# Column sums of pk: from TensorE passes with a vector of ones to block transposes on VectorE and a trip through DRAM

## The chip, the cores and the metric

The kernel runs on one core of one Trainium2 chip. The metric is the device time of one execution in microseconds (us); the median of three runs of the kernel before is 577.03 us (576.88, 577.03 and 579.19).

## What is computed

Two independent inputs, A and B, each go through the same linear attention block with S = 2048 tokens, D = 640 and 32 heads of 20 columns; the two results stand side by side in the output. Cut to one input:

```python
qkv = x @ wqkv                                   # q, k, v by heads
phi = lambda t: where(t > 0, t + 1, exp(t)) + 1e-6
pq, pk = phi(q), phi(k)
kv = einsum("bhsd,bhse->bhde", pk, v)
z  = einsum("bhsd->bhd", pk)                      # sum of pk over the tokens
num = einsum("bhqd,bhde->bhqe", pq, kv)
den = einsum("bhqd,bhd->bhq", pq, z)[..., None] + 1e-6
out = (num / den) @ wo
```

The change concerns z: for each input 640 column sums of pk over 2048 tokens. They are needed as one number per partition: z as a tile of 128 x 5, where column c holds the sums of the columns 128c to 128c+127.

## The kernel before

All large products are split into a rounded high part and a low part of float32r and cost three matmuls each (hi x hi, hi x lo, lo x hi); the projections of k and the last product go through a Strassen-like scheme of seven products (`kprod`, `outmm`).

The first half of the program (to about 293 us) makes k and its sums for A, then for B. The tokens are taken in pairs p of 128-token tiles (`("p", p, n)`: product n of pair p) and in groups i of four tiles (`("g", i, s)`, `("h", i, s, n)`: the sum of x-transposed times pk for the slice s, accumulated in PSUM and added to the SBUF tiles gacc by `gacc_add`). pk of a tile n is made from ko by `phi_exp`, `phi_relu` (ACT), `phi_mix` (DVE, L496), `phi_hi` (ACT) and `phi_lo` (DVE, L512). `phi_z` sends the 128 x 640 tile of each n to DRAM with an accumulating DMA on GpSimd's queue (zd), so that after 16 tiles zd holds, for each of 128 partitions, partial column sums over 16 tiles.

Then, for each input, `kvmm` (L648) multiplies gacc with wv for six groups of heads into a PSUM bank (pskv), `kv_mask` (DVE, L655) masks it out of the bank, `kv_hi` and `kv_lo` split it, and `mmm` multiplies it with the split wo (`o_hi` on ACT, `o_lo` on DVE, with low's line L131). The products, m, go to DRAM (md), are loaded again and combined into sums (`form_sums1`, L726, and others) for the last product. For A this lies among the k work of B; for B it lies in the second half, at the start of which the q projections begin: `qmm(u, c)` computes 128 x 512 of q for the token group u, into a PSUM bank psq, in five steps k, and after each step `run("q", u, c, k)` performs what `at(...)` put there. Three PSUM banks have the tag "one"; psq and pskv both take from it.

The order of the work is written out by hand. In the first half, steps (TensorE work, in the order of the calls, some shifted by the table MOVED) are numbered, and jobs (the other engines' work and the DMAs) are placed behind a step, some shifted by the table SHIFT; `perform` emits all in the order of these positions, a job behind the earlier created ones of the same position. Every engine and every queue performs its own instructions in exactly this order. The DMAs of loads stand on SP's queue; an instruction that waits there holds all behind it.

The column sums before: `load_z` loads zd (128 x 640) into SBUF, `zmm` makes five matmuls of it with a vector of ones into a PSUM bank psz (L609; each shows as two passes), and `z_out` adds a constant and makes the sum s of the row. For A, `load_z` stands behind ("p", 9, 2), `zmm` is a step of its own before the sums of group 4, and `z_out` follows it. For B, `load_z` stands behind ("g", 7, 7), and `zmm` and `z_out` are put at ("q", 0, 1, 0), ahead of the second `kv_step`. z is first used by `qacc` (ACT, L825) for A at the first psq of the q work, and for B four token groups later.

Of the kernel before, what the change touches and what calls it, by code (L numbers as in the profile page):

```python
# [7 lines left out]
F32 = mybir.dt.float32  # L8
# [4 lines left out]
OP = mybir.AluOpType  # L13
# [3 lines left out]
EPS = 1e-6  # L17
# [51 lines left out]
}  # L69
GROUPS = [(0, 6), (6, 6), (12, 6), (18, 6), (24, 4), (28, 4)]  # L70

# [2 lines left out]
def tile_linear_attn_pair(ctx: ExitStack, tc: tile.TileContext, ins, out: bass.AP):  # L74
# [12 lines left out]
    nc = tc.nc  # L87
    P = 128
    S, D = ins[0]["x"].shape
    NC = D // P  # L90
    NT = S // P
# [7 lines left out]
    base = ctx.enter_context(tc.tile_pool(name="base", bufs=1))  # L99
    psums = ctx.enter_context(tc.tile_pool(name="psums", bufs=1, space=bass.MemoryType.PSUM, reuse_waits="tile"))  # L100

    def bank(name, tag="one"):
        return psums.tile([P, 512], F32, name=name, tag=tag, bufs={"one": 3, "a": 2, "e": 2, "small": 1}[tag])

    dram = ctx.enter_context(tc.tile_pool(name="dram", bufs=1, space=bass.MemoryType.DRAM))
# [42 lines left out]
    def at(slot, f, *a):  # L148
        todo.setdefault(slot, []).append((f, a))
# [7 lines left out]
    wst, whl = {}, {}  # L157

    def stage(name):
        return base.tile([P, D], F32, name=name, tag="wst", bufs=7)  # L160
# [69 lines left out]
            later(1, xq_lo, u, c)  # L230


    ones = base.tile([P, 1], F32)
    epst = base.tile([P, 1], F32)
    same = base.tile([P, P], F32R)
    mask = {}
# [1 line left out]
    nc.vector.memset(epst, EPS)  # L238

    def constants():  # L240
        nc.vector.memset(ones, 1.0)
        ij = base.tile([P, P], I32, name="ij", tag="kvt", bufs=3)
        nc.gpsimd.iota(ij, pattern=[[1, P]], base=0, channel_multiplier=-1)
        nc.vector.tensor_scalar(ij, ij, H - 1, None, op0=OP.bitwise_and)
        nc.vector.tensor_scalar(same, ij, 0.0, None, op0=OP.is_equal)
        for nh in (6, 4):
            v = base.tile([P, DH * nh], F32, name=f"v{nh}", tag="kvt", bufs=3)
            m = base.tile([P, DH * nh], F32, name=f"mask{nh}")
            nc.gpsimd.iota(v, pattern=[[0, DH], [-DH, nh]], base=0, channel_multiplier=1,
                           allow_small_or_imprecise_dtypes=True)  # L250
            nc.vector.tensor_scalar(m, v, 0.0, None, op0=OP.is_ge)
            nc.vector.scalar_tensor_tensor(m, v, float(DH - 1), m, op0=OP.is_le, op1=OP.mult)
            mask[nh] = m
# [58 lines left out]
    def step(name, f, *a, after=()):  # L312
        assert name not in place, name
        place[name] = len(steps)
        steps.append((len(steps), -1, name, f, a, after))
# [7 lines left out]
    def job(name, spot, f, *a, after=()):  # L323

        spot = (place[spot] if isinstance(spot, tuple) else spot) + SHIFT.get(name, 0)
        jobs.append((spot, len(jobs), name, f, a, after))
        return spot
# [9 lines left out]
    pk, ko, zacc, gacc, kps, wf = {}, {}, {}, {}, {}, {}  # L337
# [107 lines left out]
    def prods(p, *ns):  # L445
        b = p // (NT // 2)
        for n in ns:
            after = [(k, p, x) for x in LEFT[n] for k in ("xh", "xl")]
            after += [("wf", b, i, k) for i in RIGHT[n] for k in "hl"]
            after += {2: [("c0", p)], 4: [("c2", p)], 5: [("c4", p)], 6: [("q4", p), ("p", p, 1)]}.get(n, [])  # L450
            step(("p", p, n), kprod, p, n, after=after)
# [127 lines left out]
    def gsums(i, ss, js, tags={}):  # L579
        b, g = divmod(i, NG)  # L580
        for s in ss:
            n = begun.get((i, s), 0)
            begun[i, s] = n + len(js)
            tag = tags.get(s, "one")
            step(("g", i, s) if n + len(js) == 4 else ("h", i, s, n), gsum, i, s, js, tag, n,
                 after=[(k, 4 * i + j) for j in js for k in ("nh", "nl", "ph", "pl")] + before.get((i, s), []))
            before[i, s] = [("h", i, s, n)]
# [7 lines left out]
            job(("gacc", i, s), ("g", i, s), gacc_add, i, s, after=after)  # L595


    zz, zps, md, wvt, wot, kvt, kvp, mps = {}, {}, {}, {}, {}, {}, {}, {}
    written = []

    def load_z(b):
        wst["z", b] = base.tile([P, D], F32, name="zs", tag=f"wo{'hl'[b]}", bufs=2)
        nc.sync.dma_start(wst["z", b], zacc[b])

    def zmm(b):
        x = wst["z", b]
        zps[b] = bank("psz", "small")
        for c in range(NC):
            nc.tensor.matmul(zps[b][:, c:c + 1], x[:, c * P:(c + 1) * P], ones, start=True, stop=True)  # L609

    def z_out(b):
        z = base.tile([P, NC], F32, name="z", tag="z", bufs=2)
        s = base.tile([P, 1], F32, name="zs", tag="zs", bufs=2)
        nc.vector.tensor_scalar(z, zps[b][:, :NC], S * EPS, None, op0=OP.add)
        nc.vector.tensor_reduce(s, z, axis=mybir.AxisListType.X, op=OP.add)
        nc.vector.tensor_scalar(s, s, EPS, EPS / 4, op0=OP.mult, op1=OP.add)
        zz[b] = z, s

    def z_step(b):
        zmm(b)  # L620
        z_out(b)

    def load_v(b, g):
        h0, nh = GROUPS[g]
# [327 lines left out]
    LG = NU - 1  # L952
# [41 lines left out]
    t = wst["k", 0, 0] = stage("wst")  # L994
# [24 lines left out]
    for n in first:  # L1019
        p, c = divmod(n, 2)  # L1020
# [56 lines left out]
    for i in range(NU):  # L1077
        P0, P1 = 2 * i + 1, 2 * i + 2
        if i == 0:
            gsums(i, range(2 * NC), range(4))  # L1080
        elif i in (NG - 1, LG):

            prods(P0, 0, 1, 3, 2)
            gsums(i, [0, 1], [0, 1])
            prods(P0, 4)
            gsums(i, [2], [0, 1])
            prods(P0, 5, 6)
            if i == LG:
                step(("switch",), switch, after=[("st", P0, k) for k in range(3)])
            gsums(i, range(3, 6), [0, 1], {3: "a", 4: "e", 5: "small"})  # L1090
            gsums(i, range(6), [3])
            gsums(i, range(6), [2])
            gsums(i, range(6, 2 * NC), range(4))
        elif i == NG:

            both(P0 - 1, P0)
            kvs(0)
            prods(P0, 4)
            kvs(1)
            prods(P0, 5, 6)  # L1100
            kvs(2, 3, 4, 5)
            gsums(i, range(3), [0, 1])
            step(("z",), zmm, 0, after=[("zl",)])
            gsums(i, [0], [2, 3])
            gsums(i, [1], [2, 3])
            gsums(i, [2], [2, 3])
            gsums(i, [3], range(4))
            ms(0)
            prods(P1, 0, 1, 3, 2)
            gsums(i, [4], range(4))  # L1110
            ms(1)
            prods(P1, 4)
            gsums(i, [5], range(4))
            ms(2)
            prods(P1, 5, 6)
            gsums(i, [6, 7], range(4))
            ms(3)
            gsums(i, [8], range(4))
            ms(4)
            gsums(i, [9], range(4))  # L1120
        else:
            both(P0, P1)
            gsums(i, [0], [0, 1])
            prods(P1, 4)
            gsums(i, [1, 2], [0, 1])
            prods(P1, 5, 6)
            gsums(i, range(3), [2, 3])
            gsums(i, [3], range(4))
            if i == NG + 1:
                ms(5)  # L1130
            gsums(i, range(4, 2 * NC), range(4))
# [4 lines left out]
    def h(i, s):  # L1136
        return ("h", i, s, 0)
# [18 lines left out]
    a = x_parts(1, "A2", ("c", 0, 4), [("t", 3)])  # L1156
    stores(1, 1, a + 2, ["A2"])
    a = x_parts(2, "A1", ("c", 2, 4), [("t", 4)])
    stores(2, 0, a + 2, ["A1"])
    x_parts(2, "B1", ("c", 2, 4), [("t", 5)])  # L1160
    a = x_parts(2, "A2", ("c", 3, 0), [("t", 5)])
    b = x_parts(2, "A5", ("c", 3, 0), [("t", 4), ("xh", 2, "A2")])
# [4 lines left out]
    for i in range(NU):  # L1167
# [6 lines left out]
        else:  # L1174
# [6 lines left out]
            q = P0 + 2  # L1181
# [72 lines left out]
    for g in range(NGR):  # L1254
        job(("v", g), (("p", 8, 0), ("p", 8, 1), ("p", 8, 3), ("p", 8, 2), ("p", 9, 0), ("p", 9, 1))[g], load_v, 0, g)
        a = job(("kt", g), ("kv", g), kv_mask, 0, g, after=[("kv", g)])
        job(("o", g), a, load_o, 0, g)
        a = job(("kvh", g), a, kv_hi, 0, g, after=[("kt", g)])
        job(("kvl", g), a + 1, kv_lo, 0, g, after=[("kvh", g)])
        a = job(("woh", g), (h(4, 2), ("g", 4, 3), ("p", 10, 2), ("g", 4, 5), ("g", 4, 6), ("g", 4, 8))[g], o_hi, 0, g,  # L1260
                after=[("o", g)])
        job(("wol", g), a + 0.5, o_lo, 0, g, after=[("woh", g)])
        for k, t in enumerate("ae"):
# [3 lines left out]
                       [("g", 5, 8), ("p", 14, 4)], [("g", 5, 9), h(6, 1)], ("g", 6, 4),  # L1267
                       [(0, ("p", 13, 1)), (2, ("p", 14, 0)), (6, ("p", 14, 3)), (4, h(6, 0)), (1, ("g", 6, 0)),
                        (3, ("g", 6, 2)), (5, ("g", 6, 4)), (7, ("g", 6, 5)), (8, ("p", 15, 4)), (9, ("g", 7, 0))]))
    job(("zl",), ("p", 9, 2), load_z, 0, after=[("zs", n) for n in range(NT)])  # L1270
    job(("zo",), ("z",), z_out, 0, after=[("z",)])
    job(("zl1",), ("g", LG, 7), load_z, 1, after=[("zs", n) for n in range(NT, NN)])


    for c in range(NC):
        job(("wq", c), ("p", 15, c + 1), load_w, "q", 0, c)
        a = job(("wqh", c), ("g", LG, c), wq_hi, 0, c, after=[("switch",), ("wq", c)])
# [3 lines left out]
        a = job(("xqh", c), ("g", LG, 5 + c), xq_hi, 0, c, after=[("xq", c), ("xraw", c)])  # L1281
# [8 lines left out]
           form_load, 0, i)  # L1290
    for i in range(6, 10):
        at(("q", 1, i - 5, 4) if i < 9 else ("q", 1, 4, 0), form_load, 0, i)
    at(("q", 0, 1, 0), z_step, 1)


    for g in range(NGR):
# [137 lines left out]
```

## Time and profile before

| | |
|---|---|
| median of three runs | 577.03 us |
| the profiled execution | a span of 581.2 us from the first to the last instruction; no other time of its own is given |
| TensorE (PE) busy | 571.2 us, 98% |
| VectorE (DVE) busy | 436.6 us, 75% |
| ScalarE (ACT) busy | 334.0 us, 57% |
| GpSimd (POOL) busy | 84.2 us, 14% |
| mean granted clock of TensorE | 0.993 |
| moved by DMA | 123.59 MB, 213 GB/s in the mean |

In rows of the timeline the first two numbers are the start and the duration in us; the form is out<-in by the program's names; what stands in brackets is the idle time of the engine before the instruction, and what ended it. SPq and POOLq rows are DMA issues on the queues of SyncE and GpSimd; "landing" is the time from an issue to the arrival of the data. In a row of waits stand the sum in us, the number of times and the longest. In a row of windows stand, behind the stretch, its length, the busy time (and count) of PE, PEld, DVE, ACT and POOL, the granted clock of TensorE as a share of the full one, the busy share of the DMA engines, and GB/s.

### The profile page before, as it was taken

The page shows a single profiled execution, that of the slowest core. Times are in us where ns is not written, and L with a number is a line of the kernel's source. Part 1 is how long each engine was busy: PE and PEld are TensorE (multiplying, and loading weights), DVE is VectorE, ACT ScalarE, POOL GpSimd, SP SyncE. Part 2 cuts the span into 40 slices and gives each one's busy share as a digit, 9 for nine tenths or more (in the row PEclk, how much of TensorE's full clock was granted, in tenths as well). Part 3 has the DMA queues.
Part 4 walks back from the last instruction along what each step waited for, and adds up shares of the span by engine and source line. Part 5 has one row for each costly group of instructions (what it writes and reads, how often), then busy time and mean ns, then how long its engine had stood idle before and what let it go on. Part 6 is the DMA issues. An engine that isn't in the chain of part 4 may idle for free.

```text
span 581.2 us, 9643 instructions
## 1 busy us (share of the span) xinstructions
PE 571.2 (98%) x3541; PEld 541.1 (93%) x3541; DVE 436.6 (75%) x742; ACT 334.0 (57%) x625; POOL 84.2 (14%) x139
## 2 busy tenths in 40 slices
PE   9999999999999999989989999999999999999997
PEld 7999999999999999979978889898998989898897
DVE  6897698976675778768734698977799876767792
ACT  5955757562765774736534765744647454545541
POOL 0210132310012111323200101311011200001010
PEclk9999999999999999989999999999999999999999
DMA  8879599899986958968899884764273994122022
GB/s 291 239 160 258 116 259 334 178 378 347 303 205 160 250 130 193 306 200 241 225 314 304 277 287 164 272 199 161 67 255 112 389 375 153 68 65 91 0 91 91
DMA packets 70263, 123.59 MB, mean 213 GB/s; under 512 B 7560, under 2 KB 32520, under 8 KB 70216
## 3 DMA queue, kind: packets, MB, share of 16 engines
q1 hardware_dynamic: 57912, 83.25, 44.3%
q0 software_dynamic: 12160, 39.66, 24.9%
q8 instruction: 28, 0.46, 0.3%
q14 instruction: 19, 0.16, 0.1%
q10 hardware_dynamic: 144, 0.07, 0.0%
HBM read 73.60 MB, written 49.35 MB: 212 GB/s over the span
## 4 chain that ended last, share of the span: by engine, by line
PE 52%; DMA 3%; DVE 2%; issue 0%; SPq 0%; ACT 0%; DVEq 0%
PE pa L281 12%; PE psq L142 8%; PE psq L141 8%; PE psq L143 8%; PE pe L281 6%; PE psb L281 4%; PE psg L142 2%; PE psg L143 1%; PE psg L141 1%; DMA wst<-md 1%; DMA xqs<-in_A_xt 1%; DMA zs<-zd 1%; PE pskv L648 1%; PE psd L838 0%; PE psd L837 0%
## 5 line engine op out<-in xcount | busy, mean ns | idle before, releaser
L142 PE MATMUL psg<-pkl,xnh 128*128 128x320 f32 x320 | 99.9, 312 | 2.8 <-DVE pkl L512 2.8
L141 PE MATMUL psg<-pkh,xnh 128*128 128x320 f32 x320 | 99.7, 312 | 0.0
L143 PE MATMUL psg<-pkh,xnl 128*128 128x320 f32 x320 | 99.5, 311 | 0.0
L141 PE MATMUL psq<-xqh,wqh 128*128 128x512 f32 x200 | 79.0, 395 | 0.0
L142 PE MATMUL psq<-xql,wqh 128*128 128x512 f32 x200 | 78.7, 393 | 0.0
L143 PE MATMUL psq<-xqh,wql 128*128 128x512 f32 x200 | 78.6, 393 | 0.0
L142 PEld LDWEIGHTS psg<-pkl,xnh 128*128 128x128 f32 x320 | 60.7, 190 | 3.6 <-DVE pkl L512 3.6
L143 PEld LDWEIGHTS psg<-pkh,xnl 128*128 128x128 f32 x320 | 60.7, 190 | 0.0
L141 PEld LDWEIGHTS psg<-pkh,xnh 128*128 128x128 f32 x320 | 60.6, 190 | 0.0
L285 ACT ACTIVATE o<-pa 128x320 f32<-128x320 f32 x64 | 27.9, 438 | 44.7 <-PE pa L281 44.6
L817 DVE SCALAR_TENSOR_TENSOR pq<-eq,rq 128x512 f32<-128x512 f32 x40 | 27.6, 691 | 28.3 <-ACT rq L816 28.3
L504 POOL DMA_DIRECT2D zd<-ek x30 | 26.2, 874 | 139.7 <-DVE ek L496 62.9
L285 ACT ACTIVATE ko<-pa 128x320 f32<-128x320 f32 x52 | 22.5, 435 | 41.0 <-PE pa L281 41.0
L143 PEld LDWEIGHTS psq<-xqh,wql 128*128 128x128 f32 x200 | 38.0, 190 | 8.1
L141 PEld LDWEIGHTS psq<-xqh,wqh 128*128 128x128 f32 x200 | 37.9, 189 | 7.3
L142 PEld LDWEIGHTS psq<-xql,wqh 128*128 128x128 f32 x200 | 37.9, 189 | 7.2
L815 ACT ACTIVATE eq<-psq 128x512 f32<-128x512 f32 x40 | 23.8, 596 | 33.9 <-PE psq L143 31.5
L577 DVE TENSOR_TENSOR gacc<-psg,gacc 128x320 f32<-128x320 f32 x60 | 28.6, 486 | 8.1 <-PE psg L143 8.1
L372 ACT ACTIVATE ksh<-sx 128x512 fp32r<-128x512 f32 x26 | 16.3, 628 | 30.5 <-DVE sx L390 30.4
L508 ACT ACTIVATE pkh<-ek,epst 128x640 fp32r<-128x640 f32 x32 | 26.3, 829 | 12.4 <-DVE ek L496 12.4
L496 DVE SCALAR_TENSOR_TENSOR ek<-ek,ko 128x640 f32<-128x640 f32 x32 | 26.2, 822 | 8.3 <-ACT ko L493 6.5
L134 ACT ACTIVATE dah<-pq 128x1024 fp32r<-128x1024 f32 (+5 forms) x27 | 18.2, 708 | 20.4 <-DVE pq L849 20.4
(190 smaller groups left out, 1618.2 us busy)
## 6 DMA issues: line engine op xcount, KB each, us to landing
zd<-ek POOLq DMA_DIRECT2D x32, 320.0 KB, 5.2
out<-o POOLq DMA_DIRECT2D x28, 320.0 KB, 3.2
xql<-xd SPq DMA_DIRECT2D x24, 256.0 KB, 4.4
xn<-in_A_x SPq DMA_DIRECT2D x16, 320.0 KB, 4.8
xt<-in_B_xt_tiles SPq DMA_DIRECT2D x16, 320.0 KB, 5.1
xn<-in_B_x SPq DMA_DIRECT2D x16, 320.0 KB, 5.1
xqs<-in_A_xt SPq DMA_DIRECT2D x20, 256.0 KB, 5.7
xqs<-in_B_xt SPq DMA_DIRECT2D x20, 256.0 KB, 4.5
```

The lines of the kernel that those rows point to most:

```text
L134: nc.scalar.activation(hi, src, AF.Copy)
L141: nc.tensor.matmul(o, whi, xhi, start=first, stop=False)
L142: nc.tensor.matmul(o, whi, xlo, start=False, stop=False)
L143: nc.tensor.matmul(o, wlo, xhi, start=False, stop=last)
L281: nc.tensor.matmul(o, x, y, start=start and m == r == 0, stop=m == len(terms) - 1 and r == 2, skip_group_check=True)
L285: nc.scalar.activation(x, y, AF.Copy)
L496: nc.vector.scalar_tensor_tensor(ek[n], ek[n], 1.0, rk[n], op0=OP.min, op1=OP.add)
L504: nc.gpsimd.dma_start(zacc[b], e, accum_op=OP.add)
L508: nc.scalar.activation(pk[n][0], ek[n], AF.Identity, bias=epst)
L577: nc.vector.tensor_tensor(o, sums[i, s], o, op=OP.add)
L815: nc.scalar.activation(e, ps, AF.Exp)
L817: nc.vector.scalar_tensor_tensor(pq[u][:, c, :], e, 1.0, r, op0=OP.min, op1=OP.add)
```

## The change

The matmuls with ones go, with the vector of ones and the bank psz. In their place `z_turn` transposes the loaded 128 x 640 tile on DVE in blocks of 32 x 32 (20 columns of blocks, four rows), and a DVE sum over the 32 elements of each block row gives 128 x 20 partial sums. `z_store` writes these 10 KB to DRAM in one DMA, `z_back` reads them in four DMAs of 32 partitions, in runs of five elements (20 bytes), so that the four parts of a column's sum stand on one partition, and `z_out` adds the four, then does what it did before.

For A, `load_z` moves from ("p", 9, 2) to ("p", 11, 0), and the others stand behind ("p", 12, 3), ("g", 5, 3), ("p", 14, 1) and ("g", 7, 0); the step of `zmm` is gone from the list of steps, and its shift from MOVED. The shift of `z_out` of A in SHIFT, 1.19, stays. For B, `load_z` stays, `z_turn` takes the place of `zmm` at ("q", 0, 1, 0), and the rest is put at ("q", 0, 1, 4), ("q", 0, 3, 0) and ("q", 1, 2, 1). The transposed tile takes a buffer of the other wo tag, the sums one of the three buffers kvt.

```diff
     def load_z(b):
-        wst["z", b] = base.tile([P, D], F32, name="zs", tag=f"wo{'hl'[b]}", bufs=2)
-        nc.sync.dma_start(wst["z", b], zacc[b])
-
-    def zmm(b):
-        x = wst["z", b]
-        zps[b] = bank("psz", "small")
-        for c in range(NC):
-            nc.tensor.matmul(zps[b][:, c:c + 1], x[:, c * P:(c + 1) * P], ones, start=True, stop=True)
+        zt[b] = base.tile([P, D], F32, name="zs", tag=f"wo{'hl'[b]}", bufs=2)
+        nc.sync.dma_start(zt[b], zacc[b])
+
+    def z_turn(b):
+        t = base.tile([P, D], F32, name="zt", tag=f"wo{'lh'[b]}", bufs=2)
+        nc.vector.transpose(t, zt[b])
+        zt[b] = base.tile([P, 2, 4 * NC], F32, name="zr", tag="kvt", bufs=3)
+        nc.vector.tensor_reduce(zt[b][:, 0].rearrange("p (j c) -> p c j", j=4),
+                                t.rearrange("p (c j a) -> p c j a", c=NC, j=4), axis=mybir.AxisListType.X, op=OP.add)
+
+    def z_store(b):
+        zr[b] = dram.tile([4, 32, 4 * NC], F32, name=f"zr{b}")
+        nc.sync.dma_start(zr[b].rearrange("i b c -> (i b) c"), zt[b][:, 0])
+
+    def z_back(b):
+        for j in range(4):
+            nc.sync.dma_start(zt[b][32 * j:32 * (j + 1), 1].rearrange("b (i c) -> b i c", i=4),
+                              zr[b][:, :, NC * j:NC * (j + 1)].rearrange("i b c -> b i c"))
 
     def z_out(b):
...
-        nc.vector.tensor_scalar(z, zps[b][:, :NC], S * EPS, None, op0=OP.add)
+        nc.vector.tensor_reduce(z, zt[b][:, 1].rearrange("p (i c) -> p c i", i=4),
+                                axis=mybir.AxisListType.X, op=OP.add)
+        nc.vector.tensor_scalar(z, z, S * EPS, None, op0=OP.add)
...
-            step(("z",), zmm, 0, after=[("zl",)])
...
-    job(("zl",), ("p", 9, 2), load_z, 0, after=[("zs", n) for n in range(NT)])
-    job(("zo",), ("z",), z_out, 0, after=[("z",)])
+    job(("zl",), ("p", 11, 0), load_z, 0, after=[("zs", n) for n in range(NT)])
+    job(("zt",), ("p", 12, 3), z_turn, 0, after=[("zl",)])
+    job(("zw",), ("g", 5, 3), z_store, 0, after=[("zt",)])
+    job(("zb",), ("p", 14, 1), z_back, 0, after=[("zw",)])
+    job(("zo",), ("g", LG, 0), z_out, 0, after=[("zb",)])
...
-    at(("q", 0, 1, 0), z_step, 1)
+    at(("q", 0, 1, 0), z_turn, 1)
+    at(("q", 0, 1, 4), z_store, 1)
+    at(("q", 0, 3, 0), z_back, 1)
+    at(("q", 1, 2, 1), z_out, 1)
```

More of the change, by code (lines that the diff above doesn't have):

```diff
@@ L230, in round_xq @@
             later(1, xq_lo, u, c)
-    ones = base.tile([P, 1], F32)
     epst = base.tile([P, 1], F32)
@@ L240, in constants @@
     def constants():
-        nc.vector.memset(ones, 1.0)
         ij = base.tile([P, P], I32, name="ij", tag="kvt", bufs=3)
@@ L595, in gacc_jobs @@
             job(("gacc", i, s), ("g", i, s), gacc_add, i, s, after=after)
-    zz, zps, md, wvt, wot, kvt, kvp, mps = {}, {}, {}, {}, {}, {}, {}, {}
+    zz, zt, zr, md, wvt, wot, kvt, kvp, mps = {}, {}, {}, {}, {}, {}, {}, {}, {}
     written = []
     def load_z(b):
-        wst["z", b] = base.tile([P, D], F32, name="zs", tag=f"wo{'hl'[b]}", bufs=2)
-        nc.sync.dma_start(wst["z", b], zacc[b])
-    def zmm(b):
-        x = wst["z", b]
-        zps[b] = bank("psz", "small")
-        for c in range(NC):
-            nc.tensor.matmul(zps[b][:, c:c + 1], x[:, c * P:(c + 1) * P], ones, start=True, stop=True)
+        zt[b] = base.tile([P, D], F32, name="zs", tag=f"wo{'hl'[b]}", bufs=2)
[13 more added lines that the diff above has]
+                              zr[b][:, :, NC * j:NC * (j + 1)].rearrange("i b c -> b i c"))
     def z_out(b):
@@ L617, in z_out @@
         zz[b] = z, s
-    def z_step(b):
-        zmm(b)
-        z_out(b)
     def load_v(b, g):
```

2 rows, old and new, of the table MOVED are left out of this document.

## The prediction

> **What bounds the kernel now.** I read the page first (span and busy times), then the chain of waits of TensorE, then the timeline of PE, DVE, ACT and SP around the two places where the column sums z are made, then the granted clock there.
>
> ```profile
> span 581.2 us, 9643 instructions
> PE 571.2 (98%) x3541; PEld 541.1 (93%) x3541; DVE 436.6 (75%) x742; ACT 334.0 (57%) x625; POOL 84.2 (14%) x139
> ```
> ```profile
> PE psg L142 <- DVE pkl L512: 2.8, 1, 2.8
> PE psz L609 <- DMA zs<-zd: 1.4, 1, 1.4
> PE pskv L648 <- DMA wv<-in_B_wv: 0.7, 1, 0.7
> ```
>
> TensorE is busy 571.2 of 581.2 us, and these three waits are most of the rest. So the time is PE's own instructions plus its few stalls: an instruction taken from PE counts in full, unless PE then runs into something that its delay had hidden. The profiled execution spans 581.2 us and the median of the runs shown is 577.03, so I work out a difference within the profile and add it to 577.03. Below 0.5%, 2.9 us, a measurement of this kernel hardly tells a difference from none: its three runs lie 2.3 us apart.
>
> **The passes that go.** PE's timeline, first at z of input A, then at z of input B:
>
> ```profile
> 164.25 1.21 PE L609 MATMUL psz<-ones,zs 128*128 128x1 f32 x10
> 165.32 0.39 PE L141 MATMUL psg<-pkh,xnh 128*128 128x320 f32 x1
> ```
> ```profile
> 298.90 0.39 PE L143 MATMUL psq<-xqh,wql 128*128 128x512 f32 x1
> 299.13 0.40 PE L141 MATMUL psq<-xqh,wqh 128*128 128x512 f32 x1
> 299.60 0.40 PE L143 MATMUL psq<-xqh,wql 128*128 128x512 f32 x1
> 301.42 1.28 PE L609 MATMUL psz<-ones,zs 128*128 128x1 f32 x10 [1.42 <-DMA zs<-zd]
> 302.55 1.29 PE L648 MATMUL pskv<-gacc,wv 128*120 128x120 f32 x10
> 303.60 0.55 PE L141 MATMUL psq<-xqh,wqh 128*128 128x512 f32 x1
> 307.33 1.21 PE L648 MATMUL pskv<-gacc,wv 128*120 128x120 f32 x10
> 309.78 1.21 PE L648 MATMUL pskv<-gacc,wv 128*120 128x120 f32 x10
> ```
> ```profile
> 254.00:256.00 2.00, 2.00 (x10) 2.00 (x9) 0.74 (x3) 0.74 (x1) 1.09 (x2) 0.50 0.57 149
> 304.00:306.00 2.00, 2.00 (x6) 1.60 (x5) 0.45 (x2) 0.30 (x1) 0.00 (x0) 0.50 1.03 242
> ```
>
> At A the passes hold PE from 164.25 to 165.32: 1.07 us. Nothing there waits, and until 248 the list shows no wait of PE; the only gap is one of 0.1 us at 214 (below). So I count -1.07 us.
>
> At B PE is free at 301.42 - 1.42 = 300.0, waits for zs, makes z until 302.55, and then its clock falls: column PEclk of the last fence reads 0.50 for 304 to 306. Nine psq matmuls and no more run between 303.60 and 307.33, 3.73 us; at the full clock they start 0.23 apart (298.90, 299.13), 2.1 us. So z at B costs 1.42 + 1.13 + 1.63 = 4.2 us. How much of it comes back depends on what PE meets next.
>
> **What PE meets at B.** The same stretch on the other engines: the load of wv for the second kv product, and the path of the first wo tile through ACT and DVE.
>
> ```profile
> L626 SPq DMA_DIRECT2D wv<-in_B_wv x1: 328/328/328, 294.9 to 294.9; - x1
> DMA to landing us min/median/max: 5.4/5.4/5.4
> ```
> ```profile
> 306.37 0.74 ACT L677 ACTIVATE woh<-wo 120x640 fp32r<-120x640 f32 x1 [1.87 <-DMA wo<-in_B_wo]
> 307.14 0.83 DVE L131 TENSOR_TENSOR wol<-wo,woh 120x640 fp32r<-120x640 f32 x1 [2.32 <-ACT woh L677]
> 308.58 0.28 DVE L655 TENSOR_TENSOR kvt<-pskv,mask 120x120 f32<-120x120 f32 x1 [0.61 <-PE pskv L648]
> ```
>
> Without z, the second kv product needs wv, issued at 294.9 and landed 5.4 later: it starts at 300.4, not 302.55. From there PE needs 1.05 (302.55 to 303.60) for it, 2.1 for nine psq, 1.05 for the third kv product, and 0.7 each for the last three psq of one bank and the first three of the next: 306.0. Next is the fourth kv product, which before starts at 309.78. It writes the PSUM bank of the third, so it waits until DVE has masked that one (L655). DVE stands in its queue at wol, ahead of this mask; wol waits for woh, and woh for wo, which lands at 306.3 whatever PE does. So the mask can't start before 307.14 + 0.83 = 308.0 and ends near 308.2. A second delay lies before it: z_out of A now stands in DVE's queue between the gacc adds and the wql splits that free the slots for SP's loads; its four small instructions I price at 0.5 us on the landing of wo, between 0 and 0.8. The fourth kv product starts near 308.7 instead of 309.78: -1.1 us, with PE idle for 2.7 us from 306.0.
>
> The wait that takes the place costs clock as well. Two rows bear on that: after the wait of 2.8 us near 250 the clock stood at 0.50 in 254 to 256, and after 1.42 us of waiting and 1.13 us of 128x1 passes at 0.50 in 304 to 306. The new wait is as long as either, so I take the same loss, +1.63 us, which may also be 0. The Trainium skill, TensorE: Matmul & The Clock Gate, section Why this matters for your kernels, says there should be no idle gap over about 3 us between bursts; by that rule a gap of 2.7 us keeps the clock, and the sum would be 1.63 less. The trace speaks against it: 2.8 us were enough.
>
> **z_turn, new on DVE.** A transpose and a sum over 128x640, at step ("p", 12, 3) for A and behind the first psq bank for B. No row shows a DVE transpose. DVE's rows of 640 and the dearest row by length:
>
> ```profile
> L512 DVE SCALAR_TENSOR_TENSOR pkl<-ek,pkh 128x640 fp32r<-128x640 f32 x32 | 25.9, 820 | 4.4 <-ACT pkh L508 4.4
> L843 DVE RECIPROCAL rd<-psd 128x256 f32<-128x256 f32 x16 | 27.9, 1747 | 0.9 <-PE psd L838 0.9
> ```
> ```profile
> 205.40 0.68 DVE L131 TENSOR_TENSOR ksl<-sx,ksh 128x512 fp32r<-128x512 f32 x1
> 207.24 0.82 DVE L496 SCALAR_TENSOR_TENSOR ek<-ek,ko 128x640 f32<-128x640 f32 x1 [0.20 <-ACT ko L493]
> 210.10 0.49 DVE L288 TENSOR_TENSOR ko<-pe,ko 128x320 f32<-128x320 f32 x1 [2.03 <-ACT ko L285]
> 213.22 0.83 DVE L512 SCALAR_TENSOR_TENSOR pkl<-ek,pkh 128x640 fp32r<-128x640 f32 x1 [0.17 <-ACT pkh L508]
> ```
> ```profile
> 208.40 0.31 PE L281 MATMUL pa<-wfh,ksl 128*128 128x320 f32 x1
> 214.10 0.41 PE L142 MATMUL psg<-pkl,xnh 128*128 128x320 f32 x1
> ```
> ```profile
> 199.98 0.42 SPq L349 DMA_DIRECT2D xt<-in_B_xt_tiles  x1
> DMA to landing us min/median/max: 5.3/5.6/5.9
> ```
>
> I take 0.82 each, nearest in length, 1.64 for the pair; the ends are 0.5 and 1.75 each. At A the load of z stands in SP's queue behind the xt load of 199.98, so it is issued at 200.4 and lands, with the 5.6 of the zs loads before, at 206.0. z_turn stands ahead of the ksl of 205.40: it runs to 207.65, ksl to 208.3, and PE uses ksl at 208.40. It just fits. Behind come ko, ek, then ACT's pkh and the row of 210.10, whose idle time of 2.03 us takes up most of the delay. The end is tight: the pkl of 213.22 ends at 214.05 and PE takes it at 214.10. I count +0.2 us, between 0 and 1.5; if that cover is gone, a slower transpose is paid for in full here. At B the transposed sum ends near 303.1, two us ahead of the wait for wol, and costs nothing.
>
> **z_back, new on SP.** Its four DMAs stand between the last xn load of that stretch and the loads of md at step ("p", 13, 4). The same place before:
>
> ```profile
> 241.25 2.09 SPq L165 DMA_DIRECT2D wst<-md  x3
> ```
> ```profile
> 242.44 7.12 DMA wst<-md
> ```
> ```profile
> 249.66 0.49 DVE L726 TENSOR_TENSOR t<-wst 128x320 f32<-128x320 f32 x1 [3.62 <-DMA wst<-md]
> ```
> ```profile
> 251.47 0.42 PE L142 MATMUL psg<-pkl,xnh 128*128 128x320 f32 x1 [2.78 <-DVE pkl L512]
> ```
> ```profile
> L202 SPq DMA_DIRECT2D xd<-kal x16: 370/426/1038, 10.5 to 268.1; - x16
> ```
>
> This is the longest wait of PE: SP issues the md loads at once after the xn load, DVE stands at L726 until they have landed, the pkl behind it is late, PE waits 2.78 us. Each issue put ahead of them pushes all of this back. No row shows a DMA of 20-byte runs; the nearest short-run store, xd, takes SP 0.43 us, at most 1.04. Four issues are 1.7 us; part of that lies under the queue of transfers already in flight (7.12 us to land), so I count +1.5 us, from 0.5 to 4.2. The clock is lost here before and after, for nothing more. z_store of A (13 steps earlier) and the moved load of z lie where SP has time: zero. At B SP comes to z_back near 312 and may have to wait for z_store, issued after 306, to land: with landings of 5.4 to 7 us some 1.5 us, and 1.7 for the four issues. Behind it stands the xql load for the second q group:
>
> ```profile
> 314.22 0.37 SPq L219 DMA_DIRECT2D xql<-xd  x1
> DMA to landing us min/median/max: 6.9/6.9/6.9
> ```
> ```profile
> 325.73 0.40 PE L142 MATMUL psq<-xql,wqh 128*128 128x512 f32 x1
> ```
>
> Before it lands at 321.1 and is used at 325.73: 4.6 us of cover for 3.2, so zero, and up to 1 us if z_store lands late. z_out of B comes when nobody needs it yet: zero.
>
> **Sum.** -1.07 (A's passes) + 0.2 (DVE at 206) + 1.5 (md) - 1.1 (B) + 1.63 (clock at B) = +1.2 us: 582.4 for a profile, 578.2 us for the median.
>
> **The rivals.** *The clock holds*: the gap at B falls across two of the stretches over which the clock is judged. Then 578.2 - 1.6 = 576.6 us. Against it stand both rows of 0.50; for it, that the gap is only just as long. This is where the rule of the Trainium skill cited above, TensorE: Matmul & The Clock Gate, would put the time. *Nothing stands in the way at B*: wo lands earlier, or the mask isn't behind wol any more. Then the fourth kv product starts at 306.0, 3.8 us earlier than 309.78, and no clock is lost: -1.07 + 0.2 + 1.5 - 3.8 = -3.2, 573.8 us; 572.3 if the md wait also stays as it is. For it speaks that DVE had idle time there, against it ACT's 1.87 us of waiting for wo in a stretch whose DMA share is 1.03. *z_back costs its upper end*: one mechanism, SP's queue at 241.25. If the four issues with their short runs take 1.04 us each, md lands 4.2 us later and the wait of 2.78 becomes 7: +2.7 to the sum, 580.9 us. This decides from about 3.2 us on (sum over 2.9). For it speaks that the first md issue already takes SP over 1 us, a sign that the queue is full; against it, that a full queue also hides what is put into it.
>
> **How the numbers follow.** Forecast 0.42 (its own range 576.8 to 580.2, the ends of 0.2 and of z_out's 0.5 and 1 us of md), clock holds 0.16, nothing in the way 0.16, z_back dear 0.21, the rest 0.05 (a slow transpose at 206, some 1.5 to 3 us slower). Faster by over 0.5% (under 574.1) is the third case, 0.15; slower (over 579.9) is the fourth, most of the rest and the forecast's tail, 0.28; the same, 0.57. The range from 573.4 to 581.4 leaves out the outer parts of the third and fourth case.
>
> **What would show it.** Right: PE's list of waits has pskv L648 for DVE kvt near 308 with 2 to 3 us, no psz, the wait for pkl near 252 grown to about 4.3, PEclk 0.50 behind both, and PE at the step of 214.10 at most 0.2 late against its shift. Wrong: a second kv product followed by PE without a stall (third case); a wait for pkl of 2.8 or less (md term nothing) or 6 and more (fourth); a wait of PE between 206 and 216 over 1 us (transpose dear); a wait at the start of the second q group near 325, for xql behind z_back of B on SP.

## The result and the profile after

The changed kernel takes 581.85 us in the median (580.51 to 583.64) against 577.03: ratio 1.0078, 95% interval 1.0054 to 1.0102. It is slower by 4.8 us, where 1.2 was forecast, and lies 0.45 us above the range. The times in this text are medians; the ratios are those on record, which are not quotients of two medians and differ from them by up to 0.23%.

The page of the profile after (this execution took 582.45 us), then the list of TensorE's waits:

```profile
span 580.7 us, 9624 instructions
PE 568.3 (98%) x3521; PEld 537.4 (93%) x3521; DVE 439.5 (76%) x747; ACT 334.1 (58%) x625; POOL 83.9 (14%) x139
```
```profile
PE psg L142 <- DVE pkl L510: 4.4, 3, 3.5
PE pa L279 <- ACT ko L283: 1.1, 1, 1.1
...
PE psq L142 <- DMA xql<-xd: 0.8, 1, 0.8
PE pskv L654 <- DVE kvt L661: 0.6, 1, 0.6
```

PE works 2.9 us less than in the first profile of before, and its span is only 0.5 shorter. That comparison misleads. The profiled execution took 1.75 us more than its span (582.45 and 580.7); by the same difference the first profile of before (581.2) belongs to an execution of some 583 us, 6 above the median. The kernel before, run and profiled again (c_before below), has a span of 575.2 in an execution of 576.97 us, and other waits:

```profile
PE pskv L648 <- DMA wv<-in_B_wv: 1.2, 1, 1.2
...
PE psg L142 <- DVE pkl L512: 0.7, 1, 0.7
...
PE psz L609 <- DMA zs<-zd: 0.3, 1, 0.3
```

The wait for pkl is 0.7 there, not 2.8, and the wait for zs 0.3, not 1.4. From here on "before" is this ordinary execution.

**At the md loads.** SP's queue, DVE at the first form, and PE at the pkl matmul, before and after:

```profile
240.27 2.17 SPq L165 DMA_DIRECT2D wst<-md  x3
247.30 0.49 DVE L726 TENSOR_TENSOR t<-wst 128x320 f32<-128x320 f32 x1 [1.53 <-DMA wst<-md]
249.11 0.41 PE L142 MATMUL psg<-pkl,xnh 128*128 128x320 f32 x1 [0.69 <-DVE pkl L512]
```
```profile
242.33 2.94 SPq L616 DMA_DIRECT2D zr<-zr  x4
245.31 1.42 SPq L165 DMA_DIRECT2D wst<-md  x3
252.16 0.49 DVE L732 TENSOR_TENSOR t<-wst 128x320 f32<-128x320 f32 x1 [4.37 <-DMA wst<-md]
253.97 0.41 PE L142 MATMUL psg<-pkl,xnh 128*128 128x320 f32 x1 [3.53 <-DVE pkl L510]
```

The four issues of z_back hold SP for 2.94 us. DVE stands 4.37 us at its queue's head for md instead of 1.53, and PE 3.53 instead of 0.69. Windows of before, then of after (clock, DMA share and GB/s are the last three columns):

```profile
244.00:248.00 4.00, 4.00 (x30) 4.00 (x29) 1.98 (x4) 3.66 (x7) 1.17 (x3) 1.00 1.07 308
252.00:256.00 4.00, 4.00 (x30) 4.00 (x29) 3.49 (x8) 1.25 (x2) 2.16 (x4) 1.00 0.94 285
```
```profile
244.00:248.00 4.00, 4.00 (x29) 4.00 (x29) 2.49 (x5) 3.36 (x7) 2.21 (x4) 1.00 0.75 122
252.00:256.00 4.00, 2.00 (x8) 1.74 (x9) 3.70 (x7) 0.74 (x1) 0.00 (x0) 0.84 0.75 203
```

SP puts ten kilobytes on its queue in these 2.94 us, and the DMA engines run down: 122 GB/s in 244 to 248 instead of 308. In the lowest microsecond they are busy a quarter of the time:

```profile
245.00:246.00 1.00, 1.00 (x9) 1.00 (x8) 0.17 (x1) 0.97 (x2) 1.00 (x2) 1.00 0.25 39
```

The md loads themselves are not longer on their way. From the last of their three issues to DVE's first form pass 5.9 us before, and 5.2 to 6.3 in the five profiles with z_back's four issues ahead (after, c_after, a_only, a_80, b_late; the kernels are explained below). What changes is when they leave: that last issue goes out 2.4 to 3.1 us later than before, PE's own lateness at 245 taken off. Behind the wait PE's clock falls to 0.84 in 252 to 256; before keeps 1.00.

**At the q work of B.** SP and PE after; the last row is before's issue of the same xql loads:

```profile
307.69 0.33 SPq L612 DMA_DIRECT2D zr<-zr  x1
315.25 2.59 SPq L616 DMA_DIRECT2D zr<-zr  x4
319.89 3.49 SPq L219 DMA_DIRECT2D xql<-xd  x5
325.35 0.50 PE L142 MATMUL psq<-xql,wqh 128*128 128x512 f32 x1 [0.75 <-DMA xql<-xd]
```
```profile
308.88 8.56 SPq L219 DMA_DIRECT2D xql<-xd  x5
```

SP spends 2.59 us on z_back and issues xql 11.0 us later than before. PE itself is 4.7 us late by then (the table below), so against PE the loads go out 6.3 us later, and PE waits 0.75 for them.

**Where the time went.** Each figure is the start of a TensorE matmul in a profile minus the start of the same one before, and the table gives how this shift grows across a stretch (positions in before's time). One profile is one execution; the times beside it are medians.

| | A's passes, 160 to 170 | z_turn of A, 206 to 220 | md, 245 to 258 | z and kv of B, 292 to 304.5 | xql, 318 to 330 | ratio |
|---|---|---|---|---|---|---|
| first profile of before | 0 | 0 | +3.6 | +2.1 | 0 | |
| after | -1.05 | +0.75 | +4.4 | -1.7 | +0.9 | 1.0078 |
| c_after | -1.04 | +0.87 | +5.4 | -1.7 | +3.8 | 1.0092 |
| a_only | -1.04 | 0 | +3.4 | -0.5 | 0 | 1.0062 |
| a_80 | -1.05 | +1.76 | +3.1 | -0.2 | 0 | 1.0066 |
| b_late | -1.04 | +0.21 | +3.9 | -1.3 | 0 | 1.0077 |
| a_one | -1.05 | +0.42 | -0.4 | -0.2 | 0 | 0.998 |
| ao_late | -1.04 | +0.82 | -0.1 | -1.3 | 0 | 0.999 |
| a_late | -1.04 | +0.20 | -0.2 | -2.9 | +3.7 | 0.9985 |
| ab_late | -1.05 | +0.73 | -0.2 | -2.0 | +0.3 | 0.9975 |
| b_only | 0 | 0 | -0.2 | -1.1 | +0.7 | 1.0024 |
| bo_late | 0 | 0 | -0.6 | -1.4 | 0 | 0.9985 |

The kernels are explained below. Apart from the first row, the md column divides them cleanly: +3.1 to +5.4 where four issues stand ahead of the md loads, -0.6 to -0.1 where one or none does.

The record also has the mean granted clock of every execution, so this does not rest on single profiles alone. The kernels with four issues ahead of the md loads (after, c_after, a_only, a_80, b_late) ran 37 times: in 35 the clock was 0.997 or less, and the two with 1.000 took 577.37 and 576.28 us, as long as before. Of the four kernels with A's z_back behind the md loads or in one issue, 7 of 48 executions had such a clock. Before had it too, in 14 of the 94 executions of the experiments, with a median of 579.7 us against 576.8 for the others; the execution of its first profile, with 0.993, looks like one of these. The mean clock doesn't say at which place it was lost. But a loss that hits before now and then hits nearly every execution once the four issues stand ahead.

### The profile page after: what moved, and what is told of

It is laid out like the page before. It is cut to its first block, busy times and chain, and to the rows that moved or that the text cites. A ratio compares the mean times of both kernels' runs of the same rounds, so it can differ in the third digit from the quotient of the medians.

```text
span 580.7 us, 9624 instructions
## 1 busy us (share of the span) xinstructions
PE 568.3 (98%) x3521; PEld 537.4 (93%) x3521; DVE 439.5 (76%) x747; ACT 334.1 (58%) x625; POOL 83.9 (14%) x139
## 4 chain that ended last, share of the span: by engine, by line
PE 74%; DMA 12%; DVE 7%; ACT 3%; issue 2%; SPq 1%; POOL 0%; DVEq 0%; POOLq 0%; ACTq 0%
PE pa L279 17%; PE pe L279 9%; PE psq L142 7%; PE psq L143 7%; PE psq L141 7%; PE psg L142 6%; PE psg L143 6%; PE psg L141 6%; PE psb L279 5%; DMA zd<-ek 2%; DMA wo<-in_B_wo 2%; PE psk L535 2%; DMA xn<-in_A_x 1%; DMA fh<-fdmh 1%; DMA wst<-md 1%
## 5 line engine op out<-in xcount | busy, mean ns | idle before, releaser
L131 DVE TENSOR_TENSOR xnl<-xn,xnh 128x640 fp32r<-128x640 f32 x32 | 25.7, 819 | 5.4 <-ACT xnh L414 5.0
```

The costliest lines, as they stand in the source:

```text
L131: nc.vector.tensor_tensor(lo, src, f32(hi), op=OP.subtract)
```

## The experiments

The theory (I): SP's time for z_back of A, put ahead of the md loads, costs the most, and z_back of B delays xql. The rivals: TensorE's lost stall at B and its clock (the forecast's own term); the transposes on DVE; the 20-byte runs of z_back on the DMA engines.

### Both kernels again: c_before and c_after

No edit.

> The kernel before, unchanged, for a second profile. Its first profile spans 581.2 us, while the six runs of the kernel after have spans 1.7 to 1.8 us below their times, so that the runs of before at 577.0 should have spans near 575.3. Theory P (the first profile of before was a long execution): the new span lies near 575 and the clock loss behind z at 304 (1.6 us), or the wait of 2.8 us near 250, is missing or smaller. Rival: the new span lies near 581 again and the time outside the span differs between the two kernels.

> The kernel after, unchanged. All theories: 1.005 to 1.010 of before, about 581.8 us, PE waiting for pkl near 254 by about 3.5 us and for xql near 325 by about 0.8 us as in its first profile. If the 2.0 us by which its first profile was behind before's at 120 us (ahead of anything that the change touches) come again, they belong to the kernel; if not, to that execution.

Before took 577.33 us, ratio to the runs beside it 1.0016 (0.999 to 1.0041); the changed kernel 582.66, 1.0092 (1.0058 to 1.0126). The loss repeats. The profile of c_after shows it in the same two places, larger:

```profile
PE psg L142 <- DVE pkl L510: 4.6, 2, 4.1
PE psq L142 <- DMA xql<-xd: 2.1, 1, 2.1
```
```profile
328.00:332.00 4.00, 4.00 (x14) 3.10 (x14) 2.18 (x3) 1.92 (x4) 0.00 (x0) 0.71 1.01 382
```

The wait of 2.1 us for xql is followed by a clock of 0.71, which is why this execution lost 3.8 us there and the other 0.9.

### One input at a time: a_only and b_only

```diff
 a_only: the change for A; for B as before
+    at(("q", 0, 1, 0), z_step, 1)
 b_only: the change for B; for A as before
+    job(("zl",), ("p", 9, 2), load_z, 0, after=[("zs", n) for n in range(NT)])
+            step(("z",), zmm, 0, after=[("zl",)])
```

> The change for input A alone; B keeps its TensorE passes. Theory A (z_back of A in front of the md loads is what costs): 2 to 5 us slower than before, nearly all of the loss, with the wait for pkl behind md longer by 1 us or more than in before. Theory B (the loss is at input B): within 1 us of before, or 1 us faster by the passes that are gone.

> The change for input B alone; A keeps its TensorE passes. Theory A: 0 to 3 us faster than before (z passes, the wait for zs and the clock behind it are gone, less what PE then waits for at the fourth kv product). Theory B (the wait for xql behind z_back on SP's queue and other late loads eat more than the passes cost): 2 to 5 us slower than before.

A alone took 580.28 us, ratio 1.0062 (1.0042 to 1.0083); B alone 578.26, 1.0024 (1.0004 to 1.0044). Most of the loss is A's. The SP queue, PE and windows of a_only:

```profile
239.39 1.97 SPq L634 DMA_DIRECT2D zr<-zr  x4
241.40 2.06 SPq L165 DMA_DIRECT2D wst<-md  x3
250.49 0.63 PE L142 MATMUL psg<-pkl,xnh 128*128 128x320 f32 x1 [2.95 <-DVE pkl L512]
```
```profile
240.00:244.00 4.00, 4.00 (x29) 4.00 (x28) 2.18 (x4) 3.36 (x7) 1.45 (x2) 1.00 0.71 162
248.00:252.00 4.00, 1.51 (x6) 1.51 (x7) 3.24 (x6) 1.34 (x3) 0.84 (x1) 0.79 0.98 282
```

z_back is issued at 239.39, where the md loads would have gone, and they follow 2.0 us later; PE's wait grows by 2.3. Here the DMA engines moved 162 GB/s in 240 to 244. For b_only neither expectation came true: it is 1.4 us slower, between the two. PE's list of waits names what B meets instead of z: 0.7 us for the masked bank (kvt) and 0.4 for xql.

### z_back somewhere else: a_late, b_late, ab_late

```diff
 a_late: z_back of A behind the md loads
-    job(("zb",), ("p", 14, 1), z_back, 0, after=[("zw",)])
+    job(("zb",), ("g", 6, 2), z_back, 0, after=[("zw",)])
 b_late: z_back of B behind the xql loads (and z_out of B behind it)
-    at(("q", 0, 3, 0), z_back, 1)
-    at(("q", 1, 2, 1), z_out, 1)
+    at(("q", 1, 2, 3), z_back, 1)
+    at(("q", 1, 4, 4), z_out, 1)
 ab_late: both
```

> The changed kernel with z_back of A four DMAs later on SP's queue: at step (g, 6, 2), behind all md loads, instead of in front of them. Theory A (place of z_back on SP's queue): the wait for pkl behind md falls from 3.5 to 4.1 us to about 0.7 us or less, no clock is lost behind it, and the time falls by 3 to 5 us, to 577.5 to 579. Rival R1 (the DMA rings are slowed by the short runs or by the moved load of z, wherever they stand): less than 1 us of the loss goes.

> The changed kernel with z_back of B at (q, 1, 2, 3) and its z_out at (q, 1, 4, 4), behind the loads of the second q group. Theory A: the wait for xql at the second q group (0.4 to 2.1 us in three profiles) goes, with the clock that is lost behind it when it is long: 1 to 3 us faster than the changed kernel. Rival R2 (B's loss is the wait for the masked bank at the fourth kv product, 0.3 to 0.7 us, and the DVE work): no more than 0.5 us.

> Both moves. Theory A: the passes of A (1.0 us) and of B (1.1 us and 0.3 us of waiting) are gained, 0.3 to 0.6 us are lost near 210 and as much at the fourth kv product: 0.5 to 2 us faster than before, 575 to 576.5 us. Rivals R1 and R2: still 2 us or more slower than before.

a_late took 575.38 us, ratio 0.9985 (0.9966 to 1.0004); b_late 580.0, 1.0077 (1.0049 to 1.0105); ab_late 575.88, 0.9975 (0.9954 to 0.9995). Moving A's z_back gives all of the loss back, at least 2 us more than the theory's 577.5 to 579: 1.0078 and 1.0092 become 0.9985 with nothing else touched. SP and PE of a_late:

```profile
240.54 2.51 SPq L165 DMA_DIRECT2D wst<-md  x3
243.10 2.03 SPq L616 DMA_DIRECT2D zr<-zr  x4
249.13 0.41 PE L142 MATMUL psg<-pkl,xnh 128*128 128x320 f32 x1 [0.46 <-DVE pkl L510]
```

The same four issues, 2.03 us, behind the md loads: PE waits 0.46. Moving B's alone takes the xql wait out of the list of b_late, but its time cannot be told from c_after's; the 1 to 3 us of the theory are not shown. ab_late is the one kernel whose interval lies below 1, by 0.05 to 0.46%: the change does what it can with both z_back out of the way, and that is about 1.4 us.

### Is it the runs of 20 bytes? a_80

```diff
 a_only with
-            nc.sync.dma_start(zt[b][32 * j:32 * (j + 1), 1].rearrange("b (i c) -> b i c", i=4),
-                              zr[b][:, :, NC * j:NC * (j + 1)].rearrange("i b c -> b i c"))
+            nc.sync.dma_start(zt[b][32 * j:32 * (j + 1), 1], zr[b][j])
```

> The change for input A alone, with z_back as four DMAs in the same place that read runs of 80 bytes (32 each) instead of runs of 20 bytes (128 each); the sums that come back are not the right columns, so z of A is wrong. Theory I (SP's issue time of the four DMAs delays the md loads): nothing changes against the change for A alone, 580.3 us, the wait for pkl behind md stays near 3 us. Theory S (the 512 runs of 20 bytes hold the DMA rings): md lands about 1 us earlier, the wait falls to 1 to 2 us and the clock loss may go: 577.5 to 579.

In this kernel and the next the sums of A come back in other columns than z needs, so they tell of time alone. 580.23 us, ratio 1.0066 (1.0037 to 1.0094), the same as a_only's 1.0062 with a quarter of the runs. SP's and PE's rows:

```profile
242.03 1.91 SPq L634 DMA_DIRECT2D zr<-zr  x4
243.99 2.00 SPq L165 DMA_DIRECT2D wst<-md  x3
252.51 0.42 PE L142 MATMUL psg<-pkl,xnh 128*128 128x320 f32 x1 [2.33 <-DVE pkl L512]
```

Four issues take SP 1.91 us with runs of 80 bytes and 1.97 with runs of 20. PE's wait is 0.6 us shorter than in a_only, still long enough to lose the clock (0.63 in 252 to 256), and the kernel is no faster. The short runs are not what makes it slower.

### One issue instead of four: a_one

```diff
 a_only with
-        for j in range(4):
-            nc.sync.dma_start(zt[b][32 * j:32 * (j + 1), 1].rearrange("b (i c) -> b i c", i=4),
-                              zr[b][:, :, NC * j:NC * (j + 1)].rearrange("i b c -> b i c"))
+        nc.sync.dma_start(zt[b][:, 1], zr[b].rearrange("i b c -> (i b) c"))
```

> The change for A alone, with z read back in ONE DMA in runs of 80 bytes at the same place, ahead of the md loads, instead of four (z of A comes back in wrong columns). B as before. Theory (SP's time for the issues delays the md loads): one issue of about 0.45 us instead of 1.9, so the md loads go out some 1.5 us earlier against PE; the wait for pkl near 250 falls from 3.0 to about 1.5 and mostly keeps the clock: 577 to 578, ratio 0.999 to 1.002. Rival (the place in the queue counts, or the wait of SP for something before z_back, not the number of issues): as A alone, 580.3, ratio 1.006.

576.6 us, ratio 0.998 (0.9958 to 1.0002), against 1.0062 with four issues at the same place: the intervals are apart. So the place alone costs nothing, and the bytes don't; the number of issues does.

```profile
241.45 0.73 SPq L633 DMA_DIRECT2D zr<-zr  x1
242.23 2.23 SPq L165 DMA_DIRECT2D wst<-md  x3
249.65 0.42 PE L142 MATMUL psg<-pkl,xnh 128*128 128x320 f32 x1 [0.27 <-DVE pkl L512]
```
```profile
240.00:244.00 4.00, 4.00 (x29) 4.00 (x29) 2.56 (x5) 2.86 (x6) 0.40 (x1) 1.00 1.00 372
244.00:248.00 4.00, 4.00 (x29) 4.00 (x28) 1.58 (x4) 3.66 (x7) 2.12 (x4) 1.00 0.88 232
```

The theory had left 1.5 us of wait for one issue; it was 0.27. The DMA engines stay busy: a share of 1.00 and 372 GB/s in 240 to 244, and no microsecond from there to 248 below 0.74. The last md issue goes out 0.9 us later than before against PE, but this time DVE has the data after 4.6 us instead of 5.9. A delay of 0.9 us is covered, one of 2.4 us and more isn't. That one issue is covered by the transfers already in flight is the likely reading; the trace shows the two things side by side.

### Each input alone, out of the way: ao_late and bo_late

```diff
 ao_late: a_only with z_back of A at ("g", 6, 2)
 bo_late: b_only with z_back of B at ("q", 1, 2, 3), z_out at ("q", 1, 4, 4)
```

> The change for A alone, with z_back of A behind the md loads at (g, 6, 2). B as before. Theory (z_back's place is all that A costs): A's passes are a gain of 1 us with nothing against it: 575.9, ratio 0.998, no wait for pkl over 1 us near 250; and as fast as the kernel with both moved, so that B is worth nothing. Rival (the transposes on DVE or z_store cost something too): 577 or more, ratio 1.000 or over.

> The change for B alone, with z_back of B at (q, 1, 2, 3) and z_out at (q, 1, 4, 4), behind the xql loads. A as before. Theory (B alone loses its gain of 1.5 us to the waits for the masked bank and for xql behind z_back; the second goes): about 577, ratio 0.998 to 1.001, against 1.0024 for B alone; xql waits under 0.3 us, the wait for kvt stays at 0.5 to 1.0. Rival (B's z on TensorE only filled time in which PE waits anyhow, and the xql wait isn't what costs): as B alone, 578.3, ratio 1.002.

ao_late took 577.08 us, ratio 0.999 (0.9964 to 1.0016): apart from a_only's interval, so the place of z_back is worth some 0.7%, 4 us, here too. Its profile shows the reason, no wait for pkl over 0.6; but the median is 1.2 us above what the theory gave, and 0.1 above the rival's 577; the ratio, 0.999, lies between theory and rival, and its interval holds both. In its profile +0.82 stands at z_turn, so that a part of A's gain may go there.

bo_late took 576.47 us, 0.9985 (0.9966 to 1.0005), as the theory said, against 1.0024 for B alone. The wait for xql is gone from its list of waits, and the one for the masked bank is 0.2 us, where 0.5 to 1.0 was expected.

The intervals just touch (1.0004 and 1.0005), so that z_back of B costs B's kernel time is likely rather than certain; b_late against c_after and ab_late against a_late don't show it in the times. That it makes PE wait for xql is shown in the traces: 0.4 to 2.1 us in the four profiles with z_back ahead (after, c_after, a_late, b_only), 0.3 or nothing in the three with it behind.

## Why the prediction was wrong, point by point

**The basis failed first.** The prediction worked from one profile with a span of 581.2 and added the difference to a median that belongs to spans near 575.3. The table shows what was in between: 3.6 us at md and 2.1 at z of B, stalls with lost clock that an ordinary execution doesn't have. The sentence "The clock is lost here before and after, for nothing more" hung on it, and so did the 4.2 us that z of B was to cost. Against that first profile md did grow by 0.7 (after) and 1.7 us (c_after), near the 1.5 forecast. Against an ordinary execution, to whose median the sum was added, it grew by 4.4 and 5.4.

**A's passes**, -1.07: right, -1.04 or -1.05 in all nine profiles with the change for A.

**z_turn at A**, +0.2 from 0 to 1.5: the prices were right, the landing of zs was tighter. After:

```profile
207.20 0.84 DVE L605 STREAM_TRANSPOSE zt<-zs 128x640 f32<-128x640 f32 x1 [0.71 <-DMA zs<-zd]
208.08 0.82 DVE L607 TENSOR_REDUCE zr<-zt 128x20 f32<-128x640 f32 x1
```

0.84 and 0.82 against 0.82 each. DVE waits 0.71 us for zs here. (Of the 1.2 us from the 206.0 worked out to 207.20, 1.0 is no more than the lateness of this execution against the first profile.) TensorE lost between nothing and 1.8 us in the nine profiles, 0.6 in the mean, and in each of them what DVE waited for zs at the transpose and at most 0.05 us more: nothing in a_only, 0.17 and 0.21 in b_late, 1.72 and 1.76 in a_80. So "it just fits" held for DVE's own work, and not for the load in front of it.

**md**, +1.5 from 0.5 to 4.2: the step that failed. The mechanism, the place and the time of the issues (1.97 us in a_only, with 1.7 forecast) were right; the size was not, in two parts. "Part of that lies under the queue of transfers already in flight": nothing of it did. PE's wait grew from 0.69 us to 3.53 (after), 4.14 (c_after) and 2.95 (a_only), that is by 2.8, 3.5 and 2.3 us, where the four issues took SP 2.94, 1.99 and 1.97. And the clock, thought lost anyway, is lost on top. Together the term measured +4.4 and +5.4. "Grown to about 4.3" came out for the wait, from the wrong start. The rival *z_back costs its upper end* named this queue and came to 580.9, 0.95 short; but it sought the price in 1.04 us for each issue, and each took 0.5 (a_only) to 0.7 (after), and it too saw no cost in the clock.

The Trainium skill, DMA: Bandwidth & Descriptors, section Issuing engines are not separate DMA queues, says that the time on the sequencer to start a DMA is usually small relative to the DMA itself. The rows agree for one (0.73 us in a_one, hidden) and show where it ends: four in a row, ahead of loads that the critical path waits for, were worth 4 to 5 us (1.0062 against 0.999 and 0.998).

**B**, -1.1, with PE idle for 2.7 us and +1.63 of clock: the gain was there, the gap wasn't. Up to the fourth kv product PE gains 1.1 to 2.9 us in the seven profiles with the change for B, 0.2 to 1.3 in the four without it. PE does wait for the masked bank behind wol, but for 0.2 to 1.0 us in six of the seven, since there was less to gain: z of B takes 0.33 + 1.13 = 1.5 us in an ordinary execution (the next kv product starts at 298.14), not 4.2. Before, and then the clock of after behind the new wait of 0.58 us, which ends at 308.36, where the prediction looked for 0.50:

```profile
297.01 1.28 PE L609 MATMUL psz<-ones,zs 128*128 128x1 f32 x10 [0.33 <-DMA zs<-zd]
```
```profile
308.00:312.00 4.00, 3.64 (x23) 3.35 (x24) 2.51 (x7) 1.92 (x5) 0.00 (x0) 1.00 1.03 223
```

The 1.63 us never came. The case *the clock holds* was right here, though not for its reason: the gap was short, 0.58 us and not 2.7.

**z_back of B**, zero, "up to 1 us if z_store lands late": 0.9 and 3.8. Not z_store's landing was the cause; SP's waits in after name it with less than the 1.5 us forecast:

```profile
SPq L612 <- DMA wo<-in_B_wo: 0.8, 1, 0.8
SPq L616 <- DMA zr<-zr: 0.5, 1, 0.5
```

The four issues took 2.59 us, not 1.7, and the whole edit put xql back by 6.3 us against PE, not 3.2. That is more than the cover. Before, PE uses xql at:

```profile
319.76 0.40 PE L142 MATMUL psq<-xql,wqh 128*128 128x512 f32 x1
```

From the issue at 308.88 these are 10.9 us; less the 5.5 from issue to use in after (325.35 - 319.89), 5.4 us of cover. In bo_late, with z_back behind, xql goes out at 309.99 with PE 0.8 early: 1.9 us later than before, and nobody waits. So some 4.4 of the 6.3 come with z_back, and about 1.9 with z_store and what stands around it, which the prediction had at nothing. A wait at 325 for xql was named as the sign.

**The clock.** The prediction took it that 2.8 us were enough to lose it. After the waits of 2.33 (a_80), 2.95, 3.53 and 4.14 us for pkl it fell, and after 2.07 us for xql in c_after and a_late as well; after 0.75 us (after, for xql) and 1.25 us (before, for wv near 294) it held. The row of c_after:

```profile
326.77 0.73 PE L142 MATMUL psq<-xql,wqh 128*128 128x512 f32 x1 [2.07 <-DMA xql<-xd]
```

The Trainium skill, TensorE: Matmul & The Clock Gate, section Why this matters for your kernels, puts the bound near 3 us; by these rows 2.07 can already be enough, and cost 1.7 us of clock in c_after (3.8 less the wait itself).

**Left open.** By the 160 us mark, ahead of all that the change touches, PE is 0.2 to 2.3 us late in ten of the eleven profiles of changed kernels and 0.3 in the first of before. In after, 1.2 of it follows a wait for pkl at 34 us and 1.2 a wait for ko at 120. Whether the change brings this, or it is the spread of executions, no run here tells.

## What to carry to other kernels

Count the issues that a change puts ahead of a load on the critical path, not its bytes: here one DMA of 10 KB cost nothing, and four in a row of 2.5 KB cost 4 to 5 us. A helper that ends in DMAs belongs behind the loads that somebody waits for; moved by a few steps, the same work turned from 0.8% slower to 0.25% faster. And before a difference is worked out in a profile, look whether that execution took the median's time, and which clock it had: a stall that it has by chance is neither there to be saved nor a cover for a new one.

## What was not expected of the hardware

A DVE transpose of a 128 x 640 tile of f32 in 32 x 32 blocks took 0.84 us, as long as an ordinary operation of that size (0.82). The two stores of 10 KB (z_store of A at 219.5, of B at 307.7) needed 2.3 and 7.2 us to land in after, the longer one more than the 320 KB loads of zs (5.3 to 5.9 before):

```profile
L612 SPq DMA_DIRECT2D zr<-zr x2: 327/413/499, 219.5 to 307.7; - x2
...
DMA to landing us min/median/max: 2.3/4.7/7.2
```

And reading the sums in runs of 80 bytes instead of 20 changed neither SP's time (1.91 and 1.97 us) nor the kernel's (1.0066 and 1.0062).
